# Block attention and a two-layer MLP on one core: the keys of the first batch element loaded and turned once, block means in quarters of the array

## The chip, the cores and the metric

One core of a Trainium2 chip runs the whole kernel. The metric is the time of one execution on the device in microseconds (us), the median of several runs. A core has TensorE (PE, the matrix engine; its weight loads are listed as PEld), VectorE (DVE), ScalarE (ACT), GpSimd (POOL) and SyncE (SP), which here issues all DMA transfers on one queue that 16 DMA engines serve.

## The reference

Inputs are q, k, v of shape [4 batches, 8 heads, 768 positions, 64], and two weight matrices, 512x2048 and 2048x512, all float32. For each batch and head a query sees two kinds of keys: the keys less than 16 positions away, and 24 summaries, one for each block of 32 positions.

```
k_sum = k.reshape(B, H, nb, block, D).max(axis=3)
v_sum = v.reshape(B, H, nb, block, D).mean(axis=3)
scores_l = scale * q @ k.T   where |i - j| < 16, else -1e9
scores_s = scale * q @ k_sum.T + log(32)
a = softmax(concat([scores_l, scores_s]))
x = a @ concat([v, v_sum])            # back to [3072, 512]
h = x @ w_in ; g = h - tanh(h) ; out = g @ w_out
```

## The kernel before, in words

The work is cut into 8 units: two halves of 384 positions for each batch element (unit u belongs to batch u // 2). In a unit the 8 heads are 4 pairs (p), and two pairs form a group (g) of four heads. For a pair, `prep` turns q and k so that the head dimension lies on partitions (on TensorE, against an identity matrix) and copies them out of PSUM as `qf` and `kf`; `prep_sums` writes the block maxima of the keys between the key windows in `kf`; `score` multiplies windows of 64 queries with 64 + 30 near keys and 24 block maxima; `softmax` runs on VectorE (minimum), ScalarE (exponential) and any of three engines (normalising); `transpose_probs` turns the probabilities; `value` multiplies them with `vw`, a window of value rows in which the 24 block means are placed by DMA (`put_mean`). `vw`, `rawq` and `rawk` exist once each, so the loads for the next group wait until the last reader of the group before is done.

Then come the two MLP products in 16 blocks per unit: `moe_in` (named "in"), `moe_act`, `moe_out` ("out"). Weights are loaded as two DMA transfers of 512 KB per block, and their bits rearranged by VectorE and ScalarE in `convert`. For unit 0 the products are plain float32; unit 1 uses split high and low parts; from unit 2 on "in" runs for two units at once on sums of weight blocks, which `make_sums` computes and stores to a scratch tensor (`scr`) while unit 1 is under way, and `load_sums` loads back. `make_sums` and these loads share the three buffers `wraw`.

The block maxima and means of batch 0 are made before and during unit 0. `load_part` loads whole heads of k and v; `top_pair` (the parts of k: a maximum of neighbours on VectorE, three turns on TensorE, a maximum on VectorE) and `sum_pair` (the parts of v: 12 matmuls against a matrix `blk` of 1/32, for one pair, two heads after each other in two halves of the array) followed by `place_v` (a turn of two pairs' sums, and a copy to `mean`). Batch 1 has the same functions, called in the main loop at slots 22 to 31; batches 2 and 3 use others (`sum_chunks`, `finish_k`, `finish_v`). The keys for the scores are loaded apart from these parts: by `load_qk` into `rawk`, in unit 0 as runs of four rows (turned by 8 matmuls for a pair), in later units as single rows of 256 bytes per head (turned by 4 transposes).

All of that is only declared as tasks with reads, writes and a cost for each engine that can run it. `Plan.schedule` then writes the program: it simulates the five engines and the DMA queue and always takes the ready task of highest level, where a level is the longest path to the end plus a number from a table (`BIAS` for one task, `KB` for a kind). `SL` says when a task may go to its second engine. TensorE works strictly in the order that results. Where it would idle before 100 us, `keep_warm` matmuls on the identity fill in; they show up as `pS<-ident`. At its end the program transposes a sum of squares that decides whether a second, exact version must run; with these inputs it doesn't.

Of the kernel before, what the change touches and what calls it, by code (L numbers as in the profile page):

```python
# [39 lines left out]

PREP = [0, 2, 6, 11]

TOPS = {0: [(0, 0)], 1: [(0, 2)], 3: [(0, 1)], 5: [(0, 3)]}
SUMS = {0: [(0, 0)], 1: [(0, 1)], 8: [(0, 2)], 9: [(0, 3)]}

SIGNED = set()

SL = {('g', 0, 'vector'): 4, ('g', 1, 'vector'): 0.3, ('g', 2, 'vector'): 0.6, ('g high', 0, 'vector'): -0.6, ('g high', 1, 'vector'): 2, ('g high', 2, 'vector'): 0.3, ('g low', 0, 'vector'): 0.3, ('g low', 1, 'vector'): 0.6, ('g low', 2, 'vector'): -0.3, ('k high', 0, 'vector'): 2.5, ('k high', 1, 'vector'): 0.3, ('k high', 2, 'vector'): 2, ('normal', 0, 'scalar'): -0.6, ('normal', 0, 'gpsimd'): 2, ('normal', 1, 'scalar'): 0.6, ('normal', 1, 'gpsimd'): 0, ('normal', 2, 'scalar'): 1, ('normal', 2, 'gpsimd'): -0.3, ('p out', 0, 'vector'): 0.3, ('p out', 1, 'vector'): -0.6, ('p out', 2, 'vector'): 2.5, ('part', 0, 'vector'): 2.5, ('part', 1, 'vector'): 1.5, ('part', 2, 'vector'): 0.6, ('q high', 0, 'vector'): 0, ('q high', 1, 'vector'): 4, ('q high', 2, 'vector'): -0.3, ('s high', 0, 'vector'): 0, ('s high', 1, 'vector'): 2, ('s high', 2, 'vector'): 0, ('s low', 0, 'gpsimd'): 4, ('s low', 1, 'gpsimd'): 0.3, ('s low', 2, 'gpsimd'): 2.5, ('s mix', 0, 'gpsimd'): 0.6, ('s mix', 1, 'gpsimd'): -0.3, ('s mix', 2, 'gpsimd'): 1, ('s whole', 0, 'gpsimd'): -0.6, ('s whole', 1, 'gpsimd'): 4, ('s whole', 2, 'gpsimd'): 0, ('sum guard', 0, 'gpsimd'): 2, ('sum guard', 1, 'gpsimd'): -0.6, ('sum guard', 2, 'gpsimd'): -0.6, ('top high', 0, 'scalar'): -0.6, ('top high', 1, 'scalar'): -0.3, ('top put', 0, 'vector'): 0.6, ('top put', 0, 'scalar'): 0.3, ('top put', 1, 'vector'): 0, ('top put', 1, 'scalar'): 1, ('top put', 2, 'vector'): -0.3, ('top put', 2, 'scalar'): 4, ('w high part 2', 0, 'vector'): 2.5, ('w high part 2', 1, 'vector'): 2.5, ('w high part 2', 2, 'vector'): 2.5, ('w scale', 0, 'vector'): 0.3, ('w scale', 1, 'vector'): 4, ('w scale', 2, 'vector'): 1, ('x high', 0, 'vector'): 2.5, ('x high', 1, 'vector'): 2.5, ('x high', 2, 'vector'): 2.5, ('x low', 0, 'gpsimd'): 0.3, ('x low', 1, 'gpsimd'): 1.5, ('x low', 2, 'gpsimd'): 4, ('x mix', 0, 'gpsimd'): 0.3, ('x mix', 1, 'gpsimd'): -0.6, ('x mix', 2, 'gpsimd'): 1.5, ('x whole', 0, 'vector'): 0, ('x whole', 1, 'vector'): 0.6, ('x whole', 2, 'vector'): 0.6}

KB = {('chunk load', 0): -64.2, ('chunk max', 0): 408.2, ('chunk max', 1): -8.2, ('chunk sum', 0): 144.2, ('const', 0): 299.9, ('const', 1): -136.3, ('const', 2): -50.5, ('exp', 0): -113.3, ('g', 0): -9.2, ('g high', 0): -45.7, ('g low', 0): 548.2, ('in', 0): -433.1, ('inverse', 0): 49.6, ('join', 0): 45.9, ('join', 1): -90.3, ('k high', 0): -392, ('k load', 0): 6.3, ('k load', 1): -247.1, ('k load', 2): -12.3, ('k turn', 0): -240.4, ('mean out', 0): -399.1, ('mean out', 1): -30.4, ('mean put', 0): -141.6, ('mean put', 1): 2.1, ('mean turn', 0): -385.4, ('mean turn', 1): -8.7, ('min', 0): -147.9, ('normal', 0): -47, ('out', 0): -211.9, ('p out', 0): 63.3, ('p turn', 0): -81.1, ('part', 0): 187.6, ('part', 1): -61.8, ('q high', 0): 61.1, ('q high', 1): -193.4, ('q high', 2): -481.2, ('q load', 0): -94, ('q load', 1): -130.7, ('q load', 2): -59.3, ('q turn', 0): 110.9, ('s high', 0): -19.3, ('s high', 2): 21.6, ('s load', 0): 25.8, ('s load', 1): 58.8, ('s low', 0): 611.7, ('s low', 2): 367.1, ('s mix', 0): -10.7, ('s mix', 2): 428.7, ('s store', 0): -82.7, ('s store', 2): -104.9, ('s whole', 0): 63.8, ('s whole', 2): 340, ('scores', 0): -34.8, ('seen', 0): -13.3, ('seen', 1): 313.2, ('seen', 2): 50.6, ('seen max', 0): -25.4, ('seen max', 1): -480.6, ('seen max', 2): 80.4, ('seen turn', 0): 757.5, ('seen turn', 1): 103.9, ('seen turn', 2): 276.2, ('series', 0): -293.8, ('square', 0): -596.2, ('sum', 0): 22.6, ('sum', 1): -23.8, ('sum', 2): 43.2, ('sum guard', 0): -26.5, ('sum out', 0): -77.1, ('sum out', 1): -80.2, ('sum out', 2): -476.4, ('tanh', 0): -249.6, ('tanh', 1): 1.9, ('top high', 0): 378.3, ('top high', 1): 419.7, ('top max', 0): 84.5, ('top max', 1): 350.4, ('top max', 2): 493.6, ('top pre', 0): -400.6, ('top pre', 1): 100.5, ('top pre', 2): 350.6, ('top put', 0): -275.9, ('top put', 1): -114, ('top put', 2): -73.5, ('top turn', 0): -9.3, ('top turn', 1): 424.8, ('v load', 0): -106.1, ('values', 0): 362, ('values', 1): 99.5, ('w high part 2', 0): -3.5, ('w high part 2', 1): -260.4, ('w high part 2', 2): 574.6, ('w load', 0): -332.6, ('w load', 1): -136.9, ('w load', 2): 43.5, ('w low', 0): -322.4, ('w low', 1): -17.7, ('w low', 2): -249, ('w low part 2', 0): 280.7, ('w low part 2', 1): -21.2, ('w low part 2', 2): -147.8, ('w scale', 0): 98.1, ('w scale', 1): 64.6, ('w scale', 2): -586.6, ('w shift', 0): -194.1, ('w shift', 1): 56.6, ('w shift', 2): -554.9, ('w sign', 0): -587.8, ('w sign', 1): 99, ('w sign', 2): 145, ('x high', 0): -299.8, ('x high', 1): -140.4, ('x low', 0): 123.1, ('x low', 1): -241.9, ('x mix', 0): 67.7, ('x mix', 1): -191.5, ('x whole', 0): -278.5, ('y out', 0): -64.5, ('y store', 0): -188}  # L50

HALF = {'const': (12, 12), 'k load': (33, 52), 'q load': (12, 24), 'top pre': (16, 16), 'v load': (44, 82), 'top turn': (8, 8), 'top max': (8, 8), 'q turn': (6, 15), 'q high': (12, 30), 'k turn': (6, 15), 'k high': (6, 15), 'top put': (7, 15), 'scores': (6, 14), 'sum': (8, 8), 'min': (30, 84), 'exp': (30, 84), 'sum out': (8, 8), 'sum guard': (5, 26), 'inverse': (5, 26), 'normal': (30, 84), 'p turn': (15, 42), 'p out': (15, 41), 'mean turn': (2, 4), 'mean out': (2, 4), 'mean put': (6, 14), 'values': (4, 4), 'x whole': (4, 9), 'w load': (13, 32), 'w scale': (12, 32), 'w shift': (12, 32), 'w low': (11, 32), 'w sign': (11, 32), 'w high part 2': (11, 32), 'w low part 2': (7, 32), 'in': (5, 33), 'square': (5, 33), 'tanh': (5, 32), 'series': (5, 32), 'g': (4, 32), 's store': (5, 48), 'out': (7, 96), 'x high': (0, 10), 'x low': (0, 10), 'y out': (0, 6), 'y store': (0, 6), 'g high': (0, 16), 'g low': (0, 16), 's whole': (0, 16), 's mix': (0, 32), 's high': (0, 16), 's low': (0, 16), 'chunk load': (0, 10), 'chunk max': (0, 4), 'chunk sum': (0, 4), 's load': (0, 3), 'x mix': (0, 1), 'top high': (0, 0), 'part': (0, 0), 'join': (0, 0), 'seen': (0, 0), 'seen turn': (0, 0), 'seen max': (0, 0), 'w high part': (3, 26), 'w low part': (3, 26), 'w sign 1': (4, 12), 'w sign 2': (4, 12), 'top low': (1, 2), 'cube': (2, 18), 'big': (2, 17), 'direct': (2, 17), 'pick': (2, 17), 'q low': (0, 2), 'q again': (0, 2), 'k low': (0, 2), 'k again': (0, 2)}


# [27 lines left out]
HELD = {"w shift", "w low", "w sign", "w low part", "w low part 2", "w high part", "w high part 2", "w scale", "normal", "g high", "g low", "g", "cube", "big", "top pre", "sum guard", "s whole", "s mix", "s high", "s low", "x mix", "x high", "x low"}  # L82


class Clock:


    PERIOD, ENOUGH = 10240 / 3000, 3072 / 2400
# [18 lines left out]
class Plan:  # L107
# [6 lines left out]

    SEEN = {PE: 0.2, ACT: 0.19, DVE: 0.16, POOL: 0.1, SP: 0.95}
    ISSUE = 0.5
    QUEUE = 3.0
    AHEAD = 1.1

    def __init__(self):  # L120
# [183 lines left out]
def program(  # L304
# [187 lines left out]
    def in_runs(u):  # L492

        return u < RUNS
# [872 lines left out]
```

## Time and profile before

| what | value |
|---|---|
| runs | 706.82 us median of 3 (706.42, 706.82, 714.99) |
| profiled execution | 708.19 us, of it span (first to last instruction) 706.4 us |
| mean granted TensorE clock | 0.989 of full |
| busy: PE, PEld, DVE, ACT, POOL | 678.0, 558.8, 408.9, 489.7, 250.6 us |
| DMA | 122.66 MB, 151359 packets, 58.7% of 16 engines' span |

A busy time is the sum over the instructions of an engine without double counting. A matmul's end is modelled, and matmuls overlap, so the distance of two starts says more than one duration. All instructions are issued through one helper, so they all carry line 74; they are told apart by the tiles that they write and read (out<-in). A float32 matmul that is no transpose leaves two records. "idle before <-X" is time in which the engine had nothing, and what ended it.

### The profile page before, as it was taken

To read this page: it belongs to the slowest core of one execution; us is meant where nothing else is said; L and a number is where in the kernel's file an instruction comes from. 1 tells how busy PE (TensorE), PEld (TensorE's weight loads), DVE (VectorE), ACT (ScalarE), POOL (GpSimd) and SP (SyncE) were. 2 spreads that over 40 slices of the span, in tenths; PEclk is the share of its full clock that TensorE was granted. 3 is DMA by queue.
4 is the path that set the end of the run, shared out by engine and by line. 5 is a ranking of instruction groups with operands and counts; after the bars stand their busy time and mean duration, and the time that the engine had idled before them with its cause. 6 is when DMAs were issued, how large, how long until landed. Compare 5 with 4: busy or idle time off the path is not lost. (4 is left out here: it accounts for less than half of the span.)

```text
span 706.4 us, 14180 instructions
## 1 busy us (share of the span) xinstructions
PE 678.0 (96%) x4801; PEld 558.8 (79%) x4801; DVE 408.9 (58%) x1125; ACT 489.7 (69%) x1434; POOL 250.6 (35%) x390
## 2 busy tenths in 40 slices
PE   5979999999999799999999999999999999999995
PEld 5865565569888597889878888988988889999884
DVE  3768989878877646632665665435267642222451
ACT  1755787777878666774895687676579946445882
POOL 2001211125667537441456663223236611112230
PEclk9999999999999989999999999999999999999998
DMA  8888998975564767657385647657453144345101
GB/s 200 221 228 240 275 291 245 282 245 178 158 183 138 235 213 216 169 169 195 90 232 187 167 120 199 184 174 202 159 159 116 45 150 146 123 149 165 45 1 51
DMA packets 151359, 122.66 MB, mean 174 GB/s; under 512 B 88398, under 2 KB 117102, under 8 KB 151278
## 3 DMA queue, kind: packets, MB, share of 16 engines
q1 hardware_dynamic: 151278, 121.67, 58.7%
q8 instruction: 40, 0.66, 0.4%
q14 instruction: 41, 0.34, 0.2%
HBM read 96.21 MB, written 23.07 MB: 169 GB/s over the span
## 5 line engine op out<-in xcount | busy, mean ns | idle before, releaser
L74 PE MATMUL pH<-wh,wraw 128*128 128x384 f32 x672 | 177.1, 345 | 2.4 <-DMA wraw<-scr 2.2
L74 PE MATMUL pY<-wf,gh 128*128 128x512 f32 x432 | 178.1, 440 | 0.1
L74 PE MATMUL pY<-wh,gh 128*128 128x512 f32 (+1 forms) x348 | 139.7, 406 | 0.0
L74 PE MATMUL pY<-wh,gl 128*128 128x512 f32 x336 | 132.5, 394 | 0.0
L74 PEld LDWEIGHTS pH<-wh,wraw 128*128 128x128 f32 x672 | 120.8, 189 | 12.5 <-DMA wraw<-scr 2.1
L74 POOL TENSOR_TENSOR gu<-gu,gt 128x384 f32<-128x384 f32 x52 | 53.5, 1029 | 158.5 <-ACT gu L74 131.7
L74 PE MATMUL pH<-wf,wraw 128*128 128x384 f32 x309 | 104.4, 338 | 0.0
L74 PEld LDWEIGHTS pY<-wf,gh 128*128 128x128 f32 x432 | 79.9, 189 | 22.6 <-issue 11.0
L74 ACT ACTIVATE prob<-prob,stat 128x118 f32<-128x118 f32 x232 | 86.9, 384 | 13.2 <-DVE stat L74 11.6
L74 PEld LDWEIGHTS pY<-wh,gl 128*128 128x128 f32 x336 | 63.1, 188 | 15.2
L74 PEld LDWEIGHTS pY<-wh,gh 128*128 128x128 f32 (+1 forms) x348 | 63.9, 186 | 11.4 <-issue 1.9
L74 ACT ACTIVATE gu<-gu 128x384 f32<-128x384 f32 x128 | 66.6, 521 | 1.7
L74 PE MATMUL pH<-o,wf 128*128 128x384 f32 x188 | 66.1, 450 | 1.4 <-ACT gu L74 1.4
L74 PEld LDWEIGHTS pH<-wf,wraw 128*128 128x128 f32 x309 | 58.2, 188 | 0.0
L74 ACT ACTIVATE gu<-pH 128x384 f32<-128x384 f32 x65 | 31.7, 488 | 37.1 <-PE pH L74 33.6
L74 DVE CUSTOM_DVE_ANT_0 prob<-pS,mask 128x118 f32<-128x118 f32 x180 | 40.6, 274 | 26.3 <-PE pS L74 23.8
L74 ACT ACTIVATE gv<-pH 128x384 f32<-128x384 f32 x60 | 29.2, 487 | 33.7 <-PE pH L74 33.3
L74 PEld LDWEIGHTS pH<-o,wf 128*128 128x128 f32 x188 | 35.8, 193 | 20.4 <-issue 4.5
L74 POOL COPY k<-th 64x72 f32<-64x72 f32 (+1 forms) x37 | 9.9, 266 | 97.9 <-PE pS L74 73.4
L74 POOL TENSOR_TENSOR prob<-prob,stat 128x118 f32<-128x118 f32 x75 | 35.1, 481 | 24.5 <-DVE stat L74 18.6
L74 DVE TENSOR_TENSOR gl<-gu,gh 128x384 fp32r<-128x384 f32 x41 | 25.2, 614 | 31.6 <-ACT gh L74 29.2
L74 POOL TENSOR_TENSOR gl<-gu,gh 128x384 fp32r<-128x384 f32 x29 | 31.5, 1086 | 18.0 <-ACT gh L74 12.7
(212 smaller groups left out, 1262.9 us busy)
## 6 DMA issues: line engine op xcount, KB each, us to landing
wraw<-scr SPq DMA_DIRECT2D x75, 512.0 KB
wraw<-in_moe_w_in_dram SPq DMA_DIRECT2D x16, 512.0 KB
wraw<-in_moe_w_out_dram SPq DMA_DIRECT2D x16, 512.0 KB
scr<-wraw SPq DMA_DIRECT2D x16, 512.0 KB
out_dram<-tmp SPq DMA_DIRECT2D x24, 256.0 KB
rawq<-in_q_dram SPq DMA_DIRECT2D x42, 128.0 KB
wraw<-scr SPq DMA_DIRECT2D x21, 256.0 KB
scr<-wh SPq DMA_DIRECT2D x16, 256.0 KB
```

What stands on the lines that cost most here:

```text
L74: return lambda *args, **kwargs: self._tc.keep_in_program_order(op(*args, **kwargs))
```

## The change

- **Keys of batch 0.** `all_keys` replaces `top_pair` for batch 0 and the key part of `prep` in units 0 and 1. The parts of k (whole heads, now in runs of six rows like those of v) are turned once by 2 x 12 matmuls for a pair into two PSUM banks. From them come the windows of unit 0 (`k first`, `k high`), the block maxima (`top max`, two halves) and a copy of the columns that unit 1 needs (`k keep`, into buffers of later weights); `k move` copies these into `kf` in unit 1. The loads of k by `load_qk` for units 0 and 1 go, as do their turns. `TOPS` ties the key work to the slots of `PREP`.
- **q and k in one go.** In units 2 to 7 the 3 turns of q and the 4 of k are one task.
- **Means in quarters.** `sum_pair` goes. `place_v` multiplies for a group of four heads: `blk` (now 32 columns wide) is the stationary side, the value parts the moving one, each head into its own 32 rows of PSUM, accumulated over 6 steps; four small copies bring the means to `mean`.
- `make_sums` runs after blocks 5 to 12 of unit 1 instead of 8 to 15. `transpose_probs` is written for a list of tiles but still called for one at a time.
- The costs in the plan change, `LEAVES` adds a cost to a big matmul behind a turn, and `BIAS`, `SL` and `KB` are new throughout, so that the order of tasks can change everywhere.

```diff
-TOPS = {0: [(0, 0)], 1: [(0, 2)], 3: [(0, 1)], 5: [(0, 3)]}
-SUMS = {0: [(0, 0)], 1: [(0, 1)], 8: [(0, 2)], 9: [(0, 3)]}
+TOPS = {j: [(0, n)] for n, j in enumerate(PREP)}
+SUMS = {1: [(0, 0), (0, 1)], 9: [(0, 2), (0, 3)]}
...
+    LEAVES = {"turn": 0.08, "p turn": 0.08, "scores": 0.105, "values": 0.105, "top turn": 0.17, "key turn": 0.105, "mean turn": 0.19, "sum": 0.105, "seen turn": 0.08}
...
-    do("const", DVE, 0.6, lambda: vector.memset(rawk[0:32], 0.0), w=RAWK)
-    do("const", DVE, 0.6, lambda: vector.memset(rawk[96:P], 0.0), w=RAWK)
+    do("const", DVE, 0.3, lambda: vector.memset(rawk[0:79, 0], 0.0), w=[RAWK[0]])
+    do("const", DVE, 0.3, lambda: vector.memset(rawk[96:P, 3], 0.0), w=[RAWK[3]])
+    for j in range(2):
+        do("const", DVE, 0.13, lambda j=j: vector.memset(at(("kf", j))[:, 0:79], 0.0), w=[(("kf", j), "zero")])
+    KEEP, KEPT = P * 4, (17, 19, 21, 31)
+    for p, n in enumerate(KEPT):
+        buf(("kept", p), f"wh{n}", [P, KEEP])
+        do("const", POOL, 0.2, lambda p=p: gpsimd.memset(at(("kept", p))[:, U + 79:], 0.0), w=[(("kept", p), 1)])
...
-    def sum_pair(b, p, tag):
...
+    def place_v(b, g, tag):
+        ps = bank(("mv", b, g), tag)
+        heads = [("v", b, PG * g + n // 2, n % 2) for n in range(HG)]
         def go():
+            for t in range(6):
+                for n, x in enumerate(heads):
+                    tensor.matmul(at(ps)[32 * n:32 * n + 32, :D], at(("blk",))[:, t], at(x)[:, D * t:D * (t + 1)], start=t == 0, stop=t == 5)
+        do("sum", PE, 0.8, go, r=[(x, 0) for x in heads] + [BLK], w=[(ps, 0)])
+        for n in range(HG):
+            either("mean out", {ACT: 0.2, DVE: 0.17}, lambda e, n=n: copy(e, mean[32 * g:32 * g + NB, D * n:D * (n + 1)], at(ps)[32 * n:32 * n + NB, :D]), r=[(ps, 0)], w=[MEANS[g][n]])
...
         if in_runs(u):
-            if u % 2 == 0:
-                runs(RAWK[:4], 20, 120, 0, 4)
-                runs(RAWK[4:], 19, 20, 3, 4)
...
-        if u % 2 == 0:
+        if b and u % 2 == 0:
             rows(0, 79, P)
...
-        do("q turn", PE, 0.68 if in_runs(u) else 0.285, lambda: transposes(pq, rawq, NT), r=[*RAWQ, IDENT], w=[(pq, 0)])
-        do("k turn", PE, 0.9 if in_runs(u) else 0.395, lambda: transposes(pk, rawk, 4), r=[*RAWK, IDENT], w=[(pk, 0)])
+        def turns():
+            transposes(pq, rawq, NT)
+            if u > 1:
+                transposes(pk, rawk, 4)
+        do("turn", PE, 0.8 if in_runs(u) else 0.6 if u > 1 else 0.25, turns, r=[*RAWQ, *(RAWK if u > 1 else []), IDENT], w=[(pq, 0), *([(pk, 0)] if u > 1 else [])])
...
+        elif u == 1:
+            either("k move", {ACT: 0.49, DVE: 0.4, POOL: 1.2}, lambda e: copy(e, runs(), at(("kept", p)).rearrange("p (r c) -> p r c", r=4)), r=[(("kept", p), 0), (("kept", p), 1)], w=[(kf, 0)])
+    def all_keys(p, tag):
+        kf, kept = ("kf", p % 2), ("kept", p)
+        to, n = top_base(0, p // PG), NB * (p % PG)
+        top_of[0, p] = to, [n, n]
+        st = [("k", 0, p, a) for a in range(2)]
+        for half, (r0, r1, off) in enumerate(((0, 73, 0), (50, P, U - 300))):
+            ps = bank(("ak", p, half), tag)
+            def go(ps=ps, r0=r0, r1=r1):
+                for t in range(6):
+                    for a in range(2):
+                        tensor.matmul(at(ps)[D * a:D * (a + 1), :6 * (r1 - r0)].rearrange("p (r t) -> p t r", t=6)[:, t], at(st[a])[:, D * t:D * (t + 1)], ident[:, r0:r1], start=True, stop=True)
+            do("key turn", PE, 0.9, go, r=[(x, 0) for x in st] + [IDENT], w=[(ps, 0)])
+            if half == 0:
+                either("k first", {ACT: 0.17, DVE: 0.12}, ... at(kf)[:, 79:P], at(ps)[:, :49] ...)
+                either("k high", {ACT: 0.42, DVE: 0.5}, ... at(ps)[:, 49:49 + U] ...)
+            do("top max", DVE, 0.47, ... at(ps)[:, off:off + U] ..., axis=AX.X, op=ALU.max), r=[(ps, 0)], w=[(to, p % PG)])
+            if half:
+                either("k keep", {ACT: 0.46, DVE: 0.55}, ... at(kept)[:, :U + 79], at(ps)[:, 5:468]), r=[(ps, 0)], w=[(kept, 0)])
...
-            if small_only and m[0] == 1 and m[1] >= FH:
-                make_sums(m[1] - FH)
+            if small_only and m[0] == 1 and 5 <= m[1] < FH + 5:
+                make_sums(m[1] - 5)
...
-                sum_pair(1, PG * g + n, "pH")
                 if n == 1:
                     place_v(1, g, "pS1")
```

## Rows read from the trace of the kernel before

**Rows 1.** Stretches: start:end, length, busy us of each engine, PE clock, DMA share, GB/s

```profile
60.00:100.00 40.00, 39.93 (x239) 23.54 (x238) 35.86 (x86) 29.01 (x80) 5.79 (x7) 1.00 0.88 256
100.00:155.00 55.00, 55.00 (x311) 30.18 (x309) 47.48 (x111) 41.79 (x117) 10.60 (x16) 1.00 0.90 274
155.00:240.00 85.00, 84.20 (x644) 73.87 (x642) 65.71 (x161) 66.36 (x200) 54.88 (x76) 1.00 0.57 166
240.00:256.00 16.00, 11.64 (x95) 9.11 (x95) 6.93 (x26) 9.49 (x32) 3.17 (x7) 0.79 0.82 277
```

**Rows 2.** Timeline of TensorE to 60 us: start, length, what, [idle before, its releaser]

```profile
7.90 1.55 PE L74 MATMUL pH<-ident,rawq 128*64 128x128 f32 x12 [1.29 <-DMA rawq<-in_q_dram]
11.11 1.98 PE L74 MATMUL pH<-ident,rawk 128*64 128x128 f32 x16 [1.66 <-DMA rawk<-in_k_dram]
12.84 2.30 PE L74 MATMUL pY<-wh,gu 128*64 128x24 f32 x24
15.07 1.46 PE L74 MATMUL pS<-k,q 64*64 64x118 f32 x24
...
30.35 0.87 PE L74 MATMUL pY<-probT,vw 118*64 118x64 f32 x24
...
43.95 0.92 PE L74 MATMUL pX<-probT,vw 118*64 118x64 f32 x24 [2.31 <-DMA vw<-mean]
...
46.84 2.75 PE L74 MATMUL pH<-o,wf 128*128 128x384 f32 x8
...
52.27 4.54 PE L74 MATMUL pH<-o,wf 128*128 128x384 f32 x8 [1.39 <-ACT gu L74]
```

**Rows 3.** Timeline of the sync queue's DMA issues, 31 to 42 us

```profile
31.14 6.28 SPq L74 DMA_DIRECT2D vw<-in_v_dram  x9
...
39.52 1.75 SPq L74 DMA_DIRECT2D vw<-mean  x2
```

**Rows 4.** DMA totals of the stretches 0 to 58 and 58 to 155 us

```profile
DMA packets 19137, 12.98 MB, mean 224 GB/s; under 512 B 8096, under 2 KB 18648, under 8 KB 19130
...
DMA packets 31049, 25.85 MB, mean 267 GB/s; under 512 B 12928, under 2 KB 29352, under 8 KB 31038
```

**Rows 5.** Timeline of TensorE from 72 to 252 us, columns as in Rows 2

```profile
72.89 0.60 PE L74 MATMUL pX<-ident,rawk 128*128 128x128 f32 x4
73.32 1.88 PE L74 MATMUL pY<-wf,gh 128*128 128x512 f32 x4
...
88.37 1.37 PE L74 MATMUL pH<-wh,wh 128*64 128x24 f32 x24
...
171.58 0.42 PE L74 MATMUL pH<-o,wh 128*128 128x384 f32 x1
171.84 0.34 PE L74 MATMUL pH<-o,wf 128*128 128x384 f32 x1
172.02 0.51 PE L74 MATMUL pH<-o,wh 128*128 128x384 f32 x2
...
251.44 0.63 PE L74 MATMUL pS<-vacc,ident 96*24 96x64 f32 x8
```

**Rows 6.** Timelines of VectorE and ScalarE to 30 us: key maxima and key copy

```profile
4.37 0.36 DVE L74 TENSOR_TENSOR gt<-gt 128x192 f32<-128x192 f32 x1 [0.56 <-DMA gt<-in_k_dram]
...
24.88 0.55 DVE L74 TENSOR_REDUCE th<-pH 128x24 f32<-128x384 f32 x1
...
27.47 0.57 ACT L74 ACTIVATE k<-pH 128x512 f32<-128x512 f32 x1
```

**Rows 7.** Timelines of TensorE and the sync queue from 240 to 248 us

```profile
241.13 0.55 PE L74 MATMUL pS<-ident,rawq 128*128 128x128 f32 x3 [1.93 <-DVE stat L74]
...
242.60 0.55 SPq L74 DMA_DIRECT2D scr<-wraw  x1
...
247.71 1.01 PE L74 MATMUL pH<-wh,wraw 128*128 128x384 f32 x2 [0.73 <-DMA wraw<-scr]
```

More of the change, by code (lines that the diff above doesn't have):

```diff
@@ L78 @@
     __slots__ = ("index", "costs", "go", "after", "order", "level", "count", "ready", "next", "start", "engine", "cost", "place", "out", "banks", "behind", "moves", "kind", "name")
-HELD = {"w shift", "w low", "w sign", "w low part", "w low part 2", "w high part", "w high part 2", "w scale", "normal", "g high", "g low", "g", "cube", "big", "top pre", "sum guard", "s whole", "s mix", "s high", "s low", "x mix", "x high", "x low"}
+HELD = {"w shift", "w low", "w sign", "w low part", "w low part 2", "w high part", "w high part 2", "w scale", "normal", "g high", "g low", "g", "cube", "big", "top pre", "k move", "sum guard", "s whole", "s mix", "s high", "s low", "x mix", "x high", "x low"}
 class Clock:
@@ L142, in add @@
             self.writer[key] = t
-        for base in {key[0] for key in (*r, *w)}:
+        for base in dict.fromkeys(key[0] for key in (*r, *w)):
             if base in self.first:
@@ L184, in schedule @@
         used = {}
+        left = 0.0
         def ready(t, e):
@@ L253, in schedule @@
             t.start, t.engine, t.cost = now, e, t.costs[e]
+            if e == PE:
+                t.cost += left if t.kind in ("in", "out") else 0.0
+                left = self.LEAVES.get(t.kind, 0.0)
             t.behind = [at - self.SEEN[a] for b in t.banks for a, at in used.get(b, {}).items() if a != e]
@@ L483, in program @@
     fixed(("mean",), [P, HG * D])
-    mean, MEAN = made[("mean",)], [(("mean",), g) for g in range(NG)]
+    mean = made[("mean",)]
+    MEANS = [[(("mean",), (g, n)) for n in range(HG)] for g in range(NG)]
     fixed(("rawq",), [P, NT, HG, D])
@@ L489, in program @@
     RAWQ = [(("rawq",), i) for i in range(NT)]
-    RAWK = [(("rawk",), i) for i in range(5)]
+    RAWK = [(("rawk",), i) for i in range(4)]
     def in_runs(u):
@@ L659, in top_pair @@
                    r=[(st[a], 0)] if a else (), w=[(st[0], 0)])
-        do("top turn", PE, 0.42, lambda: [tensor.transpose(at(ps)[:, P * c:P * (c + 1)], at(st[0])[:, P * c:P * (c + 1)], ident) for c in range(3)],
+        do("top turn", PE, 0.33, lambda: [tensor.transpose(at(ps)[:, P * c:P * (c + 1)], at(st[0])[:, P * c:P * (c + 1)], ident) for c in range(3)],
            r=[(st[0], 0), IDENT], w=[(ps, 0)])
@@ L801, in put_mean @@
             dma("mean put", lambda r=r, half=half: sync.dma_start(vw[r:r + NB, :, half].rearrange("r i h d -> r i (h d)"), mean[32 * g:32 * g + NB].unsqueeze(1).broadcast_to([NB, NT, HG * D])),
-                NT * NB * HG * D * 4, 1024, r=[MEAN[g]], w=[vw_keys(i, half)[2] for i in range(NT)])
+                NT * NB * HG * D * 4, 1024, r=MEANS[g], w=[vw_keys(i, half)[2] for i in range(NT)])
     def qk_of(u, p):
@@ L844, in score_keys @@
         n = qk_of(u, p)
-        return [(("qf", n), 0)] + [(("kf", n), x) for x in (0, "sums0", "sums1")]
+        return [(("qf", n), 0)] + [(("kf", n), x) for x in (0, "sums0", "sums1", *((1, "zero") if u == 0 else ()))]
     def score_of(u, p, i, a):
@@ L870, in scores_and_values @@
     def scores_and_values(now, before, tags, px_tag):
-        r, w, cost, parts = [], [], 0.13, []
+        r, w, cost, parts = [], [], 0.0, []
         if before is not None:
             px = bank(("px", *before), px_tag)
-            r, w, cost = r + value_keys(*before), w + [(px, i) for i in range(NT)], cost + 0.72
+            r, w, cost = r + value_keys(*before), w + [(px, i) for i in range(NT)], cost + 0.848
             parts.append(lambda: value(*before))
@@ L878, in scores_and_values @@
             banks = [bank(("s", u, p, n), tag) for n, tag in enumerate(tags)]
-            r, w, cost = r + score_keys(u, p), w + [(x, n) for x in banks for n in range(NT)], cost + 0.6
+            r, w, cost = r + score_keys(u, p), w + [(x, n) for x in banks for n in range(NT)], cost + 0.766
             parts.append(lambda: score(*now))
@@ L1031, in go @@
                     tensor.matmul(o, high, xl, start=False, stop=c == 1, skip_group_check=not start)
-            do("in", PE, 1.045, go, r=[(st, 0)] + [key for c in range(2) for _, key in x_of[x, u, c]], w=[(ps, 0)])
+            do("in", PE, 1.055, go, r=[(st, 0)] + [key for c in range(2) for _, key in x_of[x, u, c]], w=[(ps, 0)])
         def part(out, keys):
@@ L1063, in go @@
                     tensor.matmul(at(ph)[:, :U], at(("wf", i))[:, P * c:P * (c + 1)], at(("xf", u, c)), start=c == 0, stop=c == NC - 1)
-            do("in", PE, 2.65, go, r=[(("wf", i), 0)] + [(("xf", u, c), 0) for c in range(NC)], w=[(ph, 0)])
+            do("in first", PE, 2.62, go, r=[(("wf", i), 0)] + [(("xf", u, c), 0) for c in range(NC)], w=[(ph, 0)])
             split_whole(i)
@@ L1079, in go @@
                     tensor.matmul(o, high, xl, start=False, stop=c == NC - 1)
[L1080 removed]
+            do("in", PE, 2.095, go, r=[(st, 0)] + [key for x in xs for _, key in x], w=[(ph, 0)])
             return
@@ L1173, in go @@
                 tensor.matmul(at(y), gl, high, start=False, stop=last)
-            do("out", PE, 0.87 if whole else 0.7, go, r=keys, w=[(y, 0)])
+            do("out first" if whole else "out", PE, 0.862 if whole else 0.7, go, r=keys, w=[(y, 0)])
         if whole:
@@ L1277, in program @@
         if early:
-            for bp in tops.get(j, []):
-                if bp[0] < B and j:
-                    top_pair(*bp, "pH")
             for bp in sums.get(j, []):
```

101 lines of the change are left out of this document (45 added, 56 removed).

## The prediction, made before the changed kernel ran

> **What bounds the kernel now.** I read the windows by stage first. From 60 to 155 us TensorE is busy for the whole stretch (39.93 of 40 us, 55 of 55), while the 16 DMA engines are 88 and 90% busy and VectorE 90 and 86% [rows 1]. Three resources are thus close to full, and TensorE sets the pace only as long as the other two bring the weights in time. After 155 us only TensorE is full, except in a hole from 240 to 256 us, where it is busy 11.64 of 16 us at a granted clock of 0.79, between its two levels, 1.2 and 2.4 GHz [rows 1].
>
> Then the timeline of TensorE before 60 us, which is a chain of waits. The queries land at 7.90 us, the separately loaded keys at 11.11 (after a 1.66 us wait), the first scores run only at 15.07, behind a value sum of 2.30 us at 12.84; the second pair's values are read out at 30.35 [rows 2]. Only then can the window of values be refilled for the other four heads: nine loads occupy the sync queue for 6.28 us from 31.14, and the means are put from 39.52 [rows 3]. Values of the third pair wait for that until 43.95, and the first big matmul ("in") starts at 46.84; the second waits for ScalarE and runs at low clock, 4.54 us against 2.75 at 52.27 [rows 2]. From there on whatever comes earlier, or is not done on TensorE, comes off the end.
>
> **The change part by part.** *Keys of batch 0, traffic.* Two loads of 400 KB go (unit 0: 100 rows of 4 KB for each group of four heads), and the row loads of unit 1: 64+128+128+64+15 = 399 rows of 1 KB, once for each group, 798 KB. Together 1.6 MB. In 0 to 58 us the queue moves 224 GB/s, in 58 to 155 us 267 [rows 4]; 1.2 MB of it lies in the first stretch, 1.2/0.224 = 5.4 us, the last 0.4 MB costs 0.4/0.267 = 1.5 us. Fourteen DMA issues go with it, and nothing is put on the sync queue in their place. The key halves that were loaded for the maxima stay, in longer runs.
>
> *Keys, start of the chain.* Scores no longer wait for the second key load. The two key parts are among the first loads, so the first pair waits for the queries (7.90) and then needs a turn, a copy and a put: the turn took 1.55 us [rows 2], a copy 0.57 [rows 6], so about 10 us against 15.07, 5 us sooner. Traffic (5.4) and chain (5.1) agree; I take **-5 us** for the start of the full stage. Bounds: 0, if the value window's refill, which stays, begins no sooner for lack of value parts; -10, if the stretch from those scores to the second pair's read-out (30.35-15.07) shrinks by a third as well, another 5.1.
>
> *Keys, the work.* Per pair 24 key matmuls replace 3 maximum turns and 8 key turns; the u=1 turn (4) goes. Evacuation: before, one maximum of 0.55 us and a copy of 0.57 in each unit [rows 6], and two VectorE maxima of 0.36; after, two maxima, three copies and one move of the kept keys. By these rows (0.55, 0.57) it is 2x0.55+4x0.5 = 3.1 against 0.55+2x0.57+2x0.36 = 2.4 us per pair, +2.8 us for four, on two engines. I cost it at nothing before 47 us, where the queue waits of [rows 2] cover it; without that cover it costs half, 1.4 us, since the engines share it. The move of unit 1 falls where VectorE is at 90%, but replaces a copy of the same size. The three small copies of a group's means become four, on either engine, and the zero fills (VectorE's smaller, GpSimd's four new) lie before the queries land: nothing for both. The turn of unit 1 lies on the full TensorE: 72.89 to 73.32 [rows 5], 0.43 us, four times, **-1.7 us**.
>
> *Means in quarters.* For a group of four heads: before, two sums (1.37 us each) and a turn of four records, which I price by the four records at 72.89 (0.60) [rows 5], 3.3 us; after, 24 matmuls, 48 records, of 32 weight columns and 64 moving ones, spread over four column groups. The trace has no such form. Alone, one on the same columns after the other, 8 records of 64 moving columns took 0.63 us, 79 ns each [rows 5]; alternating between two halves, 24 records took 0.87 us, 36 ns each [rows 2]. So 48 records cost between 3.8 us (no overlap) and 0.9 us (four wide, half of 36 ns); I take the nearest row, 36 ns, 1.7 us. The Trainium skill (TensorE: Matmul & The Clock Gate, "Wait - 56ns, not 53.3ns?") says that matmul starts are never less than about 25 ns apart; by that it would be at least 1.2 us, an estimate from that page; the row's 36 ns lies above this floor, so it bears neither for nor against it. For batch 1, whose two groups lie in the full stage, 2x3.3 becomes 2x1.7; one of the four old sums stood in the wait ahead of 52.27 and cost nothing, so 6.7-1.4-3.4 = **-1.9 us** (bounds +2.3 and -3.5). Batch 0's lie in the chain above.
>
> *q and k in one go.* No instruction goes. After a turn the first matmul takes 0.26 us (171.58 to 171.84), the next 0.18 [rows 5]: leaving a turn costs 0.08 us. Of the 24 pairs of units 2 to 7 three had the two turns side by side already; 21x0.08 = **-1.7 us** (bounds 0, if they were to fill a wait, and -1.7). The Trainium skill (TensorEngine Tiling (Array Packing), Key Properties) has a drain only when the tiling mode changes; turn and matmul are both 128x128, so by that page this term would be 0. The row speaks against it: the 0.08 us is there.
>
> *Weight sums three slots sooner.* The diff also moves make_sums from blocks 8 to 15 of unit 1 to blocks 5 to 12. In the hole the last store of these sums goes out at 242.60, on a buffer ring that the next stage's weight loads share, and TensorE starts that stage at 247.71 after a wait for such a load [rows 7]. Blocks take about 85/16 = 5.3 us, so this work leaves the hole by some 16 us. What is late next is the softmax of the last pair and the split of the operands. Bounds: 0, and -6.1 (16-11.64 idle, 1.7 for the clock: half of 0.21x16, since TensorE idled through the rest); I take **-2.5 us**, well under half, since the softmax chain stays.
>
> *Given back.* The gains up to 155 us (5+1.7+1.9 = 8.6) need weights that much sooner, and traffic falls by 6.9 us only: +1.7 us. The new priorities reorder everything; I cost that at nothing, with the range.
>
> Sum: -5-1.7-1.9-1.7-2.5+1.7 = **-11.1 us** of the profiled execution's 708.19 us (span 706.4), 697.1; its runs' median is 706.82, so **696 us**.
>
> **Rivals.** *Nothing early* (chance 0.2): the refill of the value window still sets 46.84, since its nine loads and two puts stay as they are, and VectorE's 90% then holds unit 1 back. For it: the 6.28 us of issue alone. Against it: these loads wait for the second pair's read-out. Then -1.7 (joined turns) and -2.5 (hole) remain: 706.82-4.2 = 702.6; without the hole's part 705.1.
>
> *More of the holes closes* (0.27): the chain moves by 10 us, the hole at 240 closes by 6.1, and the two queues find half of what is then asked above the traffic saved ((10+1.7+1.9-6.9)/2 = 3.4 given back): 706.82-10-6.1-1.7-1.9-1.7+3.4 = 688.8, and 685.6 if the wait and the low clock at 52.27 (1.4+1.8) go as well. For it: nothing but the key load and the chain behind it holds the first scores, and VectorE and the DMA engines have 10 to 14% left [rows 1]. Against it: so much has to fit at once.
>
> *The joined turn waits* (0.06): it needs the scores' bank and the values' bank free at once, and all of q and k loaded. It is on TensorE's in-order queue, and the next matmuls stand behind it. Where both are not free, each of 24 turns would wait like the one at 241 us (1.93 us [rows 7]): 24x1.93 = 46 us at worst. It decides from 24 waits of 0.5 us on, which eat the 11 us; at 1 us each the time is 695.7+24 = 720, and from 1.1 us on it is over 2% slower. Against it: the scores of that pair need both copies anyway, and weight matmuls are at hand in most stages.
>
> *The quarters don't overlap* is a rival to the change's claim: 48 records at 79 ns, 2x(3.8-1.7) = 4.2 us more than taken for batch 1, 700 us; its chance, 0.12, is part of the forecast's case.
>
> **How the numbers follow.** The forecast's case, 693 to 701 us, has 0.47; *nothing early* 0.2 (702 to 707), *more closes* 0.27 (684 to 692), *turn waits* 0.06 (above 707). The time is that of the first. The range 686 to 706 leaves out the far ends of the first two rivals and all of the last, together some 0.18. Its terms: bounds of -10 and 0 for the start, of -6.1 and 0 for the hole, and +2.3 to -3.5 for the means. A change of under 2%, 14 us, is about what a measurement can tell from none, so faster means below 692.7: 0.3, mostly the second rival. Slower, above 721: 0.04. Within: 0.66.
>
> **What would show it.** First "in" at 42 us instead of 46.84, keys without a second load; a group's sum in 1.7 us; no key turns in unit 1; q and k turns next to each other with one exit of 0.08 us; the last store of weight sums before 230 us and TensorE busy over 13 of 16 us around 240. It is wrong if "in" still starts near 47, if VectorE leaves TensorE idle between 60 and 155 us, or if waits stand in front of the joined turns.

## The result, and the profile after

The changed kernel takes **690.02 us** (median of 4 runs, 686.08 to 691.41) against 707.7 us of the kernel before beside it (4 runs): a ratio of **0.972, 95% interval 0.964 to 0.980**, 17.7 us less. Its profiled execution took 690.38 us, of it span 688.6, at a mean granted clock of 0.993 (before 706.4 and 0.989). That lies in the predicted range of 686 to 706, but in the rival *more of the holes closes* (684 to 692) and not in the likeliest case (693 to 701, with 696 as the time). A run over 1.5% above the fastest of its kernel is left out of a ratio; that is a single run below, of 709.59 us.

The windows of the changed kernel, over the same stretches and with the columns of [rows 1]:

```profile
60.00:100.00 40.00, 40.00 (x260) 22.78 (x259) 35.31 (x79) 30.89 (x85) 7.75 (x9) 1.00 0.93 278
100.00:155.00 55.00, 55.00 (x344) 36.40 (x343) 45.27 (x109) 43.88 (x127) 11.59 (x15) 1.00 0.81 246
155.00:240.00 85.00, 85.00 (x694) 74.33 (x693) 63.51 (x189) 69.88 (x221) 44.93 (x59) 1.00 0.69 211
240.00:256.00 16.00, 14.80 (x120) 12.73 (x119) 9.53 (x37) 11.21 (x39) 7.38 (x14) 1.00 0.77 207
```

TensorE is now busy 14.80 of the 16 us from 240 on, at full clock, where it was busy 11.64 at 0.79. The stage that began with this hole, unit 2, now begins at 222.16 us (247.71 before, [rows 7]), inside a stretch without any idle time. TensorE has other work there. Before, no big matmul stands between the probabilities' turn at 237.13 and the start of the stage:

```profile
237.13 0.39 PE L74 MATMUL pS<-ident,prob 128*118 128x128 f32 x2
237.44 1.00 PE L74 MATMUL pX<-probT,vw 118*64 118x64 f32 x24
238.37 0.84 PE L74 MATMUL pS<-k,q 64*64 64x118 f32 x24
```

In the changed kernel matmuls of the second product ("out", `pY<-wh,gh`) are left over from unit 1. They stand behind the scores and the joined turn of q and k, and even behind the first "in" of unit 2 (`pH<-wh,wraw`):

```profile
217.03 0.84 PE L74 MATMUL pS<-k,q 64*64 64x118 f32 x24
217.80 0.50 PE L74 MATMUL pY<-wh,gh 128*128 128x512 f32 x1
...
220.70 0.49 PE L74 MATMUL pS<-ident,rawq 128*128 128x128 f32 x3
221.03 0.60 PE L74 MATMUL pX<-ident,rawk 128*128 128x128 f32 x4
...
222.16 0.52 PE L74 MATMUL pH<-wh,wraw 128*128 128x384 f32 x2
...
224.26 0.39 PE L74 MATMUL pY<-wh,gh 128*128 128x512 f32 x1
```

The start, as a timeline of TensorE in the changed kernel (compare [rows 2]):

```profile
4.22 1.55 PE L74 MATMUL pH<-ident,rawq 128*64 128x128 f32 x12 [0.30 <-DMA rawq<-in_q_dram]
5.55 2.19 PE L74 MATMUL pH<-ident,gt 128*64 128x73 f32 x48
...
9.03 0.84 PE L74 MATMUL pS<-k,q 64*64 64x118 f32 x24
...
25.79 0.87 PE L74 MATMUL pY<-probT,vw 118*64 118x64 f32 x24
...
35.81 0.34 PE L74 MATMUL pX<-probT,vw 118*64 118x64 f32 x4 [0.20 <-DMA vw<-mean]
...
41.08 5.33 PE L74 MATMUL pH<-o,wf 128*128 128x384 f32 x16
```

The keys are turned from their parts (gt) at 5.55, right behind the queries; the first scores stand at 9.03 instead of 15.07, the first "in" at 41.08 instead of 46.84. The issues of the sync queue (compare [rows 3]) follow:

```profile
26.35 5.97 SPq L74 DMA_DIRECT2D vw<-in_v_dram  x8
32.43 1.75 SPq L74 DMA_DIRECT2D vw<-mean  x2
```

The refill of the value window starts 4.8 us sooner and the means are put 7.1 us sooner. All loads and stores together fell from 122.66 to 121.04 MB, by the 1.6 MB of the prediction; but up to 58 us the changed kernel moved more than the one before, 14.47 MB at 250 GB/s against 12.98 at 224.

Where the 17.7 us of the two spans went, added up from the distance of each TensorE record to the start of the next one, idle time apart (worked out from both traces):

| part | us |
|---|---|
| start to the first "in" (46.84 to 41.08) | -5.8 |
| after it: sums of the means of batch 1 and their turns (6.2 to 1.6) | -4.6 |
| after it: turns of q and k (19.5 to 18.0) | -1.5 |
| after it: big matmuls of "in" and "out" (549.7 to 542.6) | -7.1 |
| after it: scores, values, turns of probabilities and the rest (0.8 of it is one pair's scores that now stand ahead of the first "in") | -1.1 |
| after it: idle (10.4 to 11.1) | +0.7 |
| from the last matmul's start to the end (7.7 to 9.2) | +1.5 |

So behind the first "in" the idle time did not fall at all. The hole at 240 has closed and others have opened; two rows of the same timeline show it:

```profile
353.94 0.27 PE L74 MATMUL pS<-ident,kacc 96*128 96x96 f32 x1 [1.86 <-DVE kacc L74]
...
383.79 0.93 PE L74 MATMUL pX<-probT,vw 118*64 118x64 f32 x24 [1.99 <-DMA vw<-mean]
```

What fell is TensorE's own time, the big matmuls' most of all, though their number is the same (2450).

### The profile page after: what moved, and what is told of

The parts are those of the page before. It is cut to its first block, busy times and chain, and to the rows that moved or that the text cites. A ratio compares the mean times of both kernels' runs of the same rounds, so it can differ in the third digit from the quotient of the medians.

```text
span 688.6 us, 14353 instructions
## 1 busy us (share of the span) xinstructions
PE 661.2 (96%) x4895; PEld 550.0 (80%) x4895; DVE 424.0 (62%) x1211; ACT 490.3 (71%) x1438; POOL 192.1 (28%) x314
## 2 busy tenths in 40 slices
DMA packets 145126, 121.04 MB, mean 176 GB/s; under 512 B 85012, under 2 KB 110868, under 8 KB 145044
## 5 line engine op out<-in xcount | busy, mean ns | idle before, releaser
L74 PE MATMUL pH<-wh,wraw 128*128 128x384 f32 x672 | 174.5, 340 | 3.0 <-DMA wraw<-scr 3.0
L74 PE MATMUL pY<-wh,gh 128*128 128x512 f32 x336 | 137.3, 408 | 0.0
L74 ACT ACTIVATE prob<-prob,stat 128x118 f32<-128x118 f32 x248 | 92.2, 384 | 13.5 <-DVE stat L74 13.0
L74 PEld LDWEIGHTS pY<-wh,gh 128*128 128x128 f32 x336 | 63.5, 189 | 11.8 <-issue 2.0
L74 PE MATMUL pH<-o,wf 128*128 128x384 f32 x188 | 64.2, 440 | 0.3 <-ACT gt L74 0.3
L74 POOL TENSOR_TENSOR gu<-gu,gt 128x384 f32<-128x384 f32 x27 | 28.7, 1063 | 112.6 <-ACT gu L74 109.7
L74 DVE TENSOR_TENSOR gu<-gu,gt 128x384 f32<-128x384 f32 x43 | 24.9, 579 | 41.2 <-ACT gu L74 40.9
L74 ACT ACTIVATE gv<-pH 128x384 f32<-128x384 f32 x54 | 26.2, 485 | 23.2 <-PE pH L74 22.5
L74 POOL TENSOR_TENSOR prob<-prob,stat 128x118 f32<-128x118 f32 x56 | 28.2, 515 | 49.3 <-DVE stat L74 33.9
L74 ACT ACTIVATE gh<-gu 128x384 fp32r<-128x384 f32 x56 | 29.2, 521 | 15.7 <-PE pY L74 12.2
```

Of the source, the lines that this page charges most:

```text
L74: return lambda *args, **kwargs: self._tc.keep_in_program_order(op(*args, **kwargs))
```

## The experiments

**The changed kernel again**, no edit, as a mark for the next three.

> The changed kernel once more, as the mark for the three kernels beside it. Every theory: 686 to 692 us, a ratio to the kernel before of 0.964 to 0.980.

688.57 us, ratio 0.9727 (0.9693 to 0.9762). The gain repeats.

**The order of the matmuls inside the mean task.**

```diff
-            for t in range(6):
-                for n, x in enumerate(heads):
+            for n, x in enumerate(heads):
+                for t in range(6):
                     tensor.matmul(at(ps)[32 * n:32 * n + 32, :D], ...)
```

> The changed kernel with the loops over heads and tiles of the batch means exchanged, so that 12 records in a row go to one column group before the next group's; the same 48 records, the same operands and the same planned cost. Theory 'the quarters overlap': a group's sum takes 48 x 79 ns = 3.8 us instead of the 0.8 seen, +3.0 us; the two groups of batch 1 lie on the full TensorE and pass it on, +6 us, those of batch 0 in the chain to the first 'in', 0 to +3. Rival 'the order is of no matter': a group's sum stays at 0.8 to 1.2 us and the time within 1.5 us. Rival 'idle time takes it': the sums grow to 3.8 us each but the time grows by less than 2 us.

691.66 us, ratio 0.9779 (0.9743 to 0.9815): 3.1 us above the mark by the medians, with intervals that overlap. This is the cleanest of the runs, since the planner sees the same task and the order on the other engines is the same. The group of batch 1 that reads the `wh` parts, by line and form (busy us, mean ns of one), in the mark's kernel and in this one:

```profile
L74 PE MATMUL pS<-wh,wh 128*32 128x64 f32 x96 | 1.8, 221 | 0.0
```

```profile
L74 PE MATMUL pS<-wh,wh 128*32 128x64 f32 x96 | 4.6, 221 | 0.0
```

And one group in the two timelines, first the changed kernel, then this one; the start of the next row says how long it held the engine:

```profile
91.84 0.88 PE L74 MATMUL pS<-wh,wh 128*32 128x64 f32 x48
92.65 1.56 PE L74 MATMUL pH<-o,wf 128*128 128x384 f32 x4
```

```profile
92.61 2.29 PE L74 MATMUL pS<-wh,wh 128*32 128x64 f32 x48
94.82 2.85 PE L74 MATMUL pH<-o,wf 128*128 128x384 f32 x8
```

0.81 us against 2.21: 17 ns a record when the four quarters alternate, 46 when one quarter's come in a row. The quarters do overlap. The starts of the single records show how (worked out from both traces): within one quarter a record starts 56 ns after the one before it; when the quarters alternate, four start 6 to 7 ns apart and the next four follow 56 ns after them. The 46 are lower than 56 because at three places one quarter's series runs into the next one's. My 79 ns was the length of a whole series, the end of its last record included, divided by eight; that series too starts a record every 56 ns. Batch 1's sums grew by 2.8 us in all, and from the first "in" to the last matmul the kernel took 3.0 us more (636.9 to 639.9); batch 0's also grew by 2.8 us, and the first "in" stayed at 41.2. In the chain the sums cost nothing; on the full TensorE they cost about what they take, as far as one trace of each can say: this kernel's has 0.7 us less idle time behind the first "in" and 3.4 us at the lower clock, which the mark's hasn't.

**The sums of the weights late again.**

```diff
-            if small_only and m[0] == 1 and 5 <= m[1] < FH + 5:
-                make_sums(m[1] - 5)
+            if small_only and m[0] == 1 and m[1] >= FH:
+                make_sums(m[1] - FH)
```

> The changed kernel with the sums of the weights back at blocks 8 to 15 of unit 1, all else kept. Theory 'the step made it': the hole at the start of unit 2 opens again by the 2.5 us of the prediction's term, at most 6; TensorE is busy for under 13 of the 16 us around 240 (shifted by what the start gained), and the last store of weight sums leaves some 16 us later. Rival 'the rest made it' (earlier start and another order): within 1.5 us of the changed kernel and the hole stays closed.

706.56 us, ratio 0.9987 (0.9962 to 1.0012): 18 us slower than the mark, beyond either theory. Windows of this kernel:

```profile
155.00:240.00 85.00, 75.74 (x635) 64.28 (x633) 63.61 (x196) 64.05 (x204) 37.38 (x55) 0.96 0.53 159
240.00:256.00 16.00, 9.05 (x73) 8.60 (x74) 6.28 (x26) 6.51 (x22) 3.33 (x8) 0.58 0.78 211
```

The hole is back and larger, and it reaches back before 240. TensorE's waits between 155 and 300 us in this kernel (total, times, longest):

```profile
PE pH L74 <- DMA wraw<-scr: 4.5, 2, 4.0
PE pX L74 <- DMA vw<-mean: 4.4, 1, 4.4
PE pS L74 <- DVE stat L74: 2.5, 1, 2.5
```

Only the first is the wait that I had put on the buffer ring; the others are the softmax chain and the value window of the same stage. The planner placed other work anew as well (TensorE's order differs from 171 us on), so this run alone does not price the step.

**The same step alone, in the kernel before**: the edit above the other way round.

> The kernel before with the sums of the weights moved to blocks 5 to 12, as the change does, and nothing else; the tables stay those of the kernel before. Theory 'late sums make the hole': 2.5 to 6 us faster, TensorE busy over 13 of the 16 us from 240. Rival 'any moved step breaks the order that the tables were made for': 5 to 30 us slower, with new holes.

710.48 us, ratio 1.0013 (0.9985 to 1.0042): nothing gained. The window of the hole and the sync queue in it:

```profile
240.00:256.00 16.00, 10.37 (x52) 8.46 (x50) 3.44 (x8) 9.00 (x28) 7.92 (x16) 0.79 0.62 198
```

```profile
244.91 0.90 SPq L74 DMA_DIRECT2D wraw<-scr  x2
245.86 0.46 SPq L74 DMA_DIRECT2D scr<-wraw  x1
```

Though they are declared three slots sooner, the last store still leaves at 245.86 (242.60 in [rows 7]). With that kernel's tables the planner takes the last of the sums late in any case: the step by itself does not move the store that the hole was put down to.

**q and k as two tasks again.**

```diff
-        def turns():
-            transposes(pq, rawq, NT)
-            if u > 1:
-                transposes(pk, rawk, 4)
-        do("turn", PE, ..., turns, ...)
+        do("turn", PE, 0.8 if in_runs(u) else 0.25, lambda: transposes(pq, rawq, NT), ...)
+        if u > 1:
+            do("k turn", PE, 0.35, lambda: transposes(pk, rawk, 4), ...)
```

> The changed kernel with the turns of q and k as two tasks again in units 2 to 7, free to be placed apart. Theory 'leaving a turn costs 0.08 us': about 21 more exits, +1.7 us, and a matmul of 0.26 us behind each of them. Rival 'it costs nothing that lasts' (the single turns fill waits, or the other order pays for itself): -1 to +0.8 us.

722.96 us, ratio 1.0218 (1.0189 to 1.0247): 34 us above the mark. Both theories miss by far. TensorE's idle time rose from 17 to 35 us, and a new hole stands behind the start of unit 2; a window of this kernel:

```profile
256.00:300.00 44.00, 36.11 (x318) 28.84 (x315) 25.27 (x97) 28.52 (x95) 17.40 (x39) 0.84 0.50 128
```

An exit of 0.08 us cannot do that; another order can.

**Both kernels with the tables empty.** After two such runs the question was how much of the gain is the tables' fit.

```diff
-BIAS = {('const', 0): -224.6, ...}
+BIAS = {}
...
-SL = {('g', 0, 'vector'): -0.3, ...}
+SL = {}
...
-KB = {('chunk load', 0): 117.2, ...}
+KB = {}
```

> The changed kernel with the three tables of the planner emptied, so that its order comes from costs and lags alone. Read as a difference to the kernel before with the same tables emptied. Theory 'the work': the difference of the two is that of the whole change, 12 to 22 us. Rival 'the tables fit this one order' (after the two runs in which a moved step cost 18 and 34 us): both bare kernels are 20 us or more slower than with their tables, and differ by under 10 us either way.

> The kernel before with the three tables emptied. Theory 'the work': 12 to 22 us slower than the changed kernel with empty tables. Rival 'the tables fit this one order': 725 us or more, and within 10 us of the bare changed kernel.

The changed kernel 740.72 us, ratio 1.0446 (1.0387 to 1.0506); the kernel before 755.94 us, ratio 1.0665 (1.0605 to 1.0725). The tables are worth 48 us in the kernel before and 51 in the changed one. The difference between the two kernels stays: 15.2 us by the medians; by the ratios 0.0219 of 707, with the two intervals combined 15.5 +-6 us. Most of the gain is thus not the tables'; the rest, some 2.5 us, is not told from zero. What is left is the work together with the planner's new costs (`LEAVES` among them), which no run takes apart, each in one order. Added up as above, the two bare traces differ by 2.9 us up to the first "in", 3.9 in the means, 2.8 in the turns of q and k and 4.2 in the big matmuls. What the big matmuls took longer in stretches at the lower clock fell by 4.7 us alone (6.4 to 1.7), and big matmuls behind a turn of q or k are nearly as many in both (28 and 23). So there the means and the turns are worth about what they are in the tuned kernels, the start half, and the big matmuls' part is the clock's, which one trace of each does not make a lasting one.

**The two steps that moved most, without tables**: the late sums, and the two turns, each in the changed kernel with empty tables.

> The changed kernel with empty tables and the sums of the weights at blocks 8 to 15; to be held against the changed kernel with empty tables (740.7 us). Theory 'the step has its own worth': 2.5 to 6 us slower. Rival 'the 18 us were a misfit of the tables': within 2.5 us of it either way, or faster.

> The changed kernel with empty tables and the turns of q and k as two tasks; to be held against the changed kernel with empty tables (740.7 us). Theory 'the exit of a turn': +1.7 us. Theory 'the joined turn orders the work better by itself': +5 us or more. Rival 'the 34 us were a misfit of the tables': within 4 us of it either way.

742.69 us, ratio 1.0492 (1.0446 to 1.0538), and 746.45 us, ratio 1.054 (1.050 to 1.058), against 740.72. The late sums cost 2.0 us by the medians and 3.3 by the ratios (0.0046 +-0.0076 of 707: -2 to +9), which decides between neither of the two theories; the two turns cost 5.7 us (by the ratios 0.0094 +-0.0071: 2 to 12). More than half of the 18 us was a misfit of the tables even at the upper end of the interval, and so were at least 22 of the 34. Whether what is left of the turns is more than the exits is open.

**One key load back in unit 0, with and without a reader.** The load of 100 rows of 4 KB for each group; in the first kernel one record reads it ahead of the turn of q, in the second nothing does and two table entries put it early. In both it is the fourth load on the queue, at 2.31 us.

```diff
+            extra = k[b, hs, t0:t0 + 400].rearrange("h (r t) d -> r h (t d)", t=4)
+            dma("extra load", lambda: sync.dma_start(by_runs(rawk, 4)[0:100]..., extra), ..., w=RAWK)
...
         def turns():
+            if in_runs(u):
+                tensor.matmul(at(pq)[:D, :P], by_runs(rawk, 4)[0:100, hs.start, 0], ident[0:100], ...)
```

> The changed kernel with one key load of 400 KB for each group of unit 0 put back, and one record that reads it ahead of the turn of q of each pair, so that the first scores wait for it as they did before; what the record computes is overwritten. Theory 'chain': the first scores move back from 9 us by 2 to 4, the first 'in' from 41 to 44 to 46 us, and the time by 3 to 6 us. Theory 'traffic': the first 'in' moves by 0.8 MB at 0.224 MB per us, 3.6 us, as well, but also in the kernel that loads the same and waits for nothing. Rival 'order': 10 us or more, from holes after 155 us.

698.73 us (the median of five runs; a sixth took 709.59), ratio 0.9847 (0.9792 to 0.9902), 8.7 us more than the changed kernel's 690.02. TensorE's timeline in this kernel:

```profile
10.26 0.45 PE L74 MATMUL pH<-ident,rawk 100*64 100x128 f32 x1 [4.29 <-DMA rawk<-in_k_dram]
...
16.93 0.84 PE L74 MATMUL pS<-k,q 64*64 64x118 f32 x24
...
48.72 3.71 PE L74 MATMUL pH<-o,wf 128*128 128x384 f32 x11
```

> The changed kernel with one key load of 400 KB for each group of unit 0 put back early on the sync queue, and nothing that reads it. The kernel that also waits for it had its first 'in' 7.6 us later and took 9.7 us more. Theory 'chain': without the wait the first 'in' is within 1.5 us of 41.1 and the time within 3 us of 690. Theory 'traffic': 0.8 MB at 0.224 MB per us, the first 'in' 3.6 us later and the time 3 to 5 us longer. Rival 'order': 8 us or more, with new holes after 155 us.

715.97 us, ratio 1.012 (1.0079 to 1.016). The timeline of TensorE in the kernel that only loads:

```profile
9.78 0.84 PE L74 MATMUL pS<-k,q 64*64 64x118 f32 x24
...
43.03 8.02 PE L74 MATMUL pH<-o,wf 128*128 128x384 f32 x24
```

Up to the first "in" the load alone costs 1.95 us (43.03 against 41.08), the wait for it another 5.7 (48.72). The chain is most of what the keys held up; 0.8 MB of traffic cost about half of the 3.6 us that the rate gives. The 5.7 are not the wait alone: the granted clock fell to its lower level at 9.16 us, within the 4.29 us of idle time, and stayed there until 15.99, while the kernel that only loads ran at full clock. The same stretch in the first kernel and in the second:

```profile
9.00:16.00 7.00, 5.74 (x66) 5.38 (x68) 1.25 (x3) 1.22 (x4) 0.00 (x0) 0.51 0.73 191
```

```profile
9.00:16.00 7.00, 6.82 (x169) 5.57 (x170) 5.30 (x30) 4.56 (x18) 0.00 (x0) 1.00 0.89 239
```

The wait put back is also the harder one: the first "in" comes later than before the change (48.72 against 46.84). Of the time at the end the two kernels say little: the one with less to wait for is 17 us slower, so there the order of the rest decides, as the third theory has it.

**The earlier queries and identity, in the kernel before.** Two entries of its table, ahead of loads and constants:

```diff
-BIAS = {('const', 0): -1245, ... ('q load', 0): -1579.7, ...
+BIAS = {('const', 0): 2000, ... ('q load', 0): 1939.8, ...
```

> The kernel before with two entries of its table raised, so that the load of the queries is issued first and the identity is made first, as in the changed kernel; the keys are still loaded apart and turned after the queries. Theory 'the key load holds the scores': the first scores stay at 14 to 15.5 us, the first 'in' within 1.5 us of 46.8, the time within 4 us of 707. Rival 'the tables made the earlier start': first scores at 11 us or sooner, first 'in' at 43 or sooner, 3 us or more faster.

706.65 us, ratio 0.9997 (0.9965 to 1.0029). The timeline of TensorE in this kernel:

```profile
9.21 1.95 PE L74 MATMUL pH<-ident,rawk 128*64 128x128 f32 x16 [1.74 <-DMA rawk<-in_k_dram]
...
13.12 1.46 PE L74 MATMUL pS<-k,q 64*64 64x118 f32 x24
...
45.78 2.75 PE L74 MATMUL pH<-o,wf 128*128 128x384 f32 x8
```

Neither theory holds whole: the first scores come 1.95 us sooner (13.12), more than the first allowed and less than the second wanted, the first "in" 1.06 us sooner, and the time is the same. About a fifth of the start's 5.8 us is thus the order of two small things that the tables brought, perhaps more: this kernel's trace is at the lower clock from 9.27 to 16.10 us, which that of the kernel before is not. The rest I put down to the keys, by subtraction and by the two kernels above; without tables the whole start is worth 2.9 us, so part of it may be the new order of the rest.

## Why the prediction was right or wrong

The range held, and the forecast of 696 us was 6 too high. That comes from terms that missed in both directions: the start and the turns about as forecast, the means 2.7 us better, the big matmuls better by what no term held, the hole's gain lost elsewhere. That the sum still lies in the range is owed to its width. I gave 0.3 to a gain clear of what a measurement can tell from none, and it is such a gain.

*Start of the full stage, -5 us.* Right in size (-5.8) and, for the larger part, in mechanism. I had two reasons that agreed, traffic (5.4) and chain (5.1). The kernels with the load put back tell them apart: 1.95 us without the wait, 5.7 more with it. The argument from traffic took 224 GB/s for a limit, but the changed kernel moves 250 in the same stretch; its agreement with the chain was chance. What I did not see is that the queries could land sooner than 7.90, since the new tables put their load and the identity first: about 1.1 us of the 5.8.

*Key turns of unit 1 and joined turns, -1.7 and -1.7.* The turns themselves take 1.5 us less. The exits are found in the big matmuls behind them: where one follows a turn of q or k, the distance to the next start is longer by a median of 0.086 us than where it follows its own kind (0.084 after); there were 45 such places and are 24 (52 and 27 exits, the others into turns of probabilities), and the extra time summed over them falls from 5.0 to 2.5 us. Together -4.0 us against -3.4. The Trainium skill (TensorEngine Tiling (Array Packing), Key Properties) names a drain for a change of tiling mode and none within a mode; by that alone there would be no exit to save. Both traces show one at every such place, 0.078 us or more.

*Means in quarters, -1.9 us.* Measured -4.6, the term that was sized worst. Two things in it failed. The price: I took the row of two alternating halves, 36 ns a record, as nearest; four quarters took 17, half of that, just below the lower bound of 0.9 us for a group (0.81), which I had worked out and passed over. And the credit of 1.4 us for a sum that "stood in the wait ahead of 52.27": nothing of it stayed in the result, since TensorE's work after the first "in" fell by the whole of the old sums and turns (6.2 us) but the 1.6. The Trainium skill (TensorE: Matmul & The Clock Gate, "Wait — 56ns, not 53.3ns?") has starts never less than about 25 ns apart, which gave the estimate of 1.2 us; the measured 0.81 us is below that, and the trace has records of different quarters start 6 to 7 ns apart, so for four quarters the measurement decides.

*Weight sums three slots sooner, -2.5 us for the hole.* The hole did close (idle 4.36 to 1.20 us, clock 0.79 to 1.00), but the step named does not do it alone: in the kernel before it gained nothing, and there the last store left no sooner. With the changed kernel's order the sums do leave early, the last within these two:

```profile
214.09 2.62 SPq L74 DMA_DIRECT2D scr<-wraw  x2
```

Putting them late brings the hole back; in an order without tables the same move costs 2.0 us, not told from none. So the hole closes by the new order as a whole, as far as the rows tell: it keeps "out" matmuls of unit 1 for the time of the softmax chain and can start unit 2 among them, since the weight sums are there. With the sums late again no big matmul stands between 228.1 and 249.9 us, where unit 2 then starts. No run tests this reading by itself. I had ascribed to one line what a line and an order did together. And of the time it brought nothing by itself: 3.2 us less idle there, 0.7 more in all.

*Given back, +1.7 us.* The size came out (0.7 us of idle time and a tail 1.5 us longer), the mechanism did not, so this is luck: the term was for weights that come too late before 155 us, and TensorE waits for nothing from 60 to 155 us. What was given back lies at later stage starts and behind the last matmul.

*What was missing* is the rest of the big matmuls' 7.1 us. About 2.5 are the exits of the turns of q and k and 0.6 those of the probabilities' turns (55 to 45). Of the other 4, the clock is the largest part: before, it stood at its lower level for some 10 us (3.4 from 52.9 and 6.8 from 244 us), after for 3.4. The big matmuls that touch these stretches were together 4.1 us longer than the median of their form before, and 1.5 after: 2.5 us. The mark bears this out: the same kernel, with no such stretch ahead of its tail, and big matmuls of 541.2 us against 542.6. I had this price in the rival (1.4+1.8 us at 52.27) and, for the hole, in its bound. It was worked out from the records and not tried in a kernel of its own.

*The rivals.* *Nothing early* falls: the first "in" moved. *The joined turn waits* falls: a row like that at 241 us is seen at the joined turns only once, 1.20 us for the queries, at 254.58. *The quarters don't overlap* falls by the 2.2 against 0.8 us. *More of the holes closes* gives the time nearly (688.8 against 690.0) but not the way: I had the chain 10 us shorter and the idle time filled; what happened is a chain shorter by 5.8, no less idle time behind it, and 14 us less of TensorE's own time, the lower clock's 2.5 among it. That the likelier number stood with this rival is luck.

*Open* is what each step is worth in a well-ordered kernel. The runs with a moved task changed the order of all that follows, and cost 9 to 34 us in the changed kernel, against nothing in two edits of the kernel before; only the edit within one task is free of that.

## What to carry to other kernels

Where a planner with tuned tables writes the order, undoing one step in the tuned kernel measures how well the tables fit, not the step: edit within one task, or compare both kernels with the tables empty. On an engine that is full, count what each task holds it, start to next start and with the slower matmul behind it, rather than its waits; the waits moved here, and the work that was gone stayed gone. When two arguments give the same number, as traffic and chain did, the number says nothing on which is true.

## What the runs showed of the hardware

Matmuls of 32 weight columns and 64 moving ones took 17 ns a record when four column quarters alternated, and 46 ns when twelve records in a row went to the same quarter (0.81 and 2.21 us for 48 records): with the same operands and number, the order of the loops alone makes a factor of 2.7. In both orders a quarter started a record every 56 ns; alternating, four quarters did so at once, 6 to 7 ns apart. A big matmul behind a turn of q or k is 0.085 us longer by the median, at 45 places before and 24 after. Two executions of the changed kernel, one with 3.4 us at the lower clock ahead of its tail and one without, differ by 1.4 us in their big matmuls.
